# Both gates of a gated feed-forward layer by seven block products instead of eight, with the steps behind attention in a written order

## Chip, core and metric

The kernel runs on one core of a Trainium2 chip. The metric is device time in microseconds (us) of one execution; of several executions the median counts.

## What is computed

Attention with rotary positions (2 batches, 8 heads, 576 positions, 64 per head), a gated layer, and a layer with a softmax-weighted activation and a normalisation. Cut to what matters:

```python
x = attention(q, k, v)                 # as 1152 rows of 512
a = x @ w_a                            # 512 -> 1536
b = x @ w_b                            # 512 -> 1536
x = (a * b) @ w_out                    # 1536 -> 512
h = x @ w_in                           # 512 -> 1024
e = np.exp(h - np.max(h, axis=-1, keepdims=True))
solu = h * (e / (np.sum(e, axis=-1, keepdims=True) + 1e-09))
ln = (solu - mean(solu)) / np.sqrt(var(solu) + 1e-06) * g_ln
return ln @ w_out2                     # 1024 -> 512
```

The weights arrive as 64-bit floats.

## The kernel before

**Precision.** Each operand of a matmul is split into a high part (rounded to the matmul's own float32 form) and a low part (the rest); a product is three matmuls, high by high, high by low and low by high, summed in PSUM.

**Weights.** A 64-bit weight tile is loaded on SP's queue into `raw` (two staging buffers, each with its `f`), and `pack` makes a float32 tile of its bits in five steps: step 0 (L89, absolute value) on ACT; step 1 (L91, clip to a range), step 2 (L93, shift), step 3 (L95, sign) and step 4 (L97, low bits) on DVE. `high` (L103) rounds on ACT, `low` (L106) subtracts on POOL or on DVE. A staging buffer is loaded again when step 4 has read it.

**Attention** (up to about 167 us) runs by positions in a table (`PLAN` and its variants); what interests here is that it ends with `x_last`, which writes the last columns of `xT`: four tiles of 128 features by 1152 positions, high and low. The two batches are columns 0 to 575 and 576 to 1151. The first two of twelve weight blocks, and eight of the matmul triples of block 0, stand inside that table.

**Gates** (L629 to L646). The 1536 columns of `w_a` and `w_b` are cut in 12 blocks of 128. For block `f` and column third `t` (384 positions) one group of 24 matmuls fills two PSUM banks: 2 gates, 4 feature tiles, 3 matmuls each. ACT copies gate a out (L637), DVE multiplies it by gate b (L638), ACT and DVE split the product into `gT` (L645, L646). Two groups are open at a time. Steps of later weight blocks are dealt out between the groups.

**The second matmul** (L745): for each of 4 output tiles and each third, all 12 blocks are summed, 36 matmuls of 384 columns in a row; `x2_out` splits the result. **The last layer**: `hmm` (L792, 24 matmuls of 512 columns for each of 9 row tiles), a chain of maximum, exponential, product, statistics and norm, four-fold transposes (L834), the output matmuls (L863) and the stores. Here the order is written out by hand.

Engines take their instructions in the order of the program; a step waits by semaphores for what it reads and for the buffer that it writes.

Of the kernel before, what the change touches and what calls it, by code (L numbers as in the profile page):

```python
# [75 lines left out]
class Weights:  # L76
# [3 lines left out]
    def __init__(self, nc, raw, t, w, scale=None):  # L80
        self.nc, self.raw, self.t, self.w, self.scale = nc, raw, t, w, scale

    def pack(self, steps=range(5)):

        eng, t = self.nc.vector, self.t
        lo, hi = self.raw[:, :, 0], self.raw[:, :, 1]
        for step in steps:
            if step == 0:
                self.nc.scalar.activation(_raw(t), _raw(hi), AF.Abs)  # L89
            elif step == 1:  # L90
                eng.tensor_scalar(_raw(t), _raw(t), LOW_END, HIGH_END, op0=ALU.max, op1=ALU.min)  # L91
            elif step == 2:
                eng.tensor_scalar(t, t, 3, 0x3FFFFFFF, op0=ALU.logical_shift_left, op1=ALU.bitwise_and)  # L93
            elif step == 3:
                eng.scalar_tensor_tensor(t, hi, -(1 << 30), t, op0=ALU.bitwise_and, op1=ALU.bitwise_or)  # L95
            else:
                eng.scalar_tensor_tensor(t, lo, 29, t, op0=ALU.logical_shift_right, op1=ALU.bitwise_or)  # L97

    def high(self):
        t = _raw(self.t)  # L100
        if self.scale is not None:
            self.nc.scalar.activation(t, t, AF.Copy, scale=self.scale)
        self.nc.scalar.copy(self.w[:, 0], t)  # L103
# [6 lines left out]
def attention_gated_ffn_solu_ffn(ctx: ExitStack, tc, q, k, v, wa, wb, wo1, wi2, wo2, gln, rope_cs, out):  # L110
# [17 lines left out]
    W, wt = {}, {}  # L128
# [7 lines left out]
    def load_w(key, w, raw, t):  # L136
        kind, n = key
        scale = None
        if kind == "ab":
            rv = raw.rearrange("p (m k c) t -> p m k (c t)", m=2, k=4)  # L140
            for m, src in enumerate((wa, wb)):
                nc.sync.dma_start(
                    out=rv[:, m], in_=src[:, 2 * n * P:2 * (n + 1) * P].rearrange("(k p) c -> p k c", p=P)
                )
        elif kind == "x":
            m, half = divmod(n, 2)
            raw, t = raw[:, :6 * P], t[:, :6 * P]
            nc.sync.dma_start(
                out=raw.rearrange("p (f c) t -> p f (c t)", f=6),
                in_=wo1[half * 6 * P:(half + 1) * 6 * P, 2 * m * P:2 * (m + 1) * P].rearrange("(f p) c -> p f c", p=P),  # L150
            )
        else:
            half = slice(n % 2 * DM, (n % 2 + 1) * DM)
            raw, t, w = raw[:, half], t[:, half], w[:, :, half]
            if kind == "h":
                t = staged[n // 4][:, n % 4]
                src = wi2[n // 2 * P:(n // 2 + 1) * P, n % 2 * 2 * DM:(n % 2 + 1) * 2 * DM]
            else:
                src, scale = wo2[n * P:(n + 1) * P, :], g_sb[:, n:n + 1]
            nc.sync.dma_start(out=raw.rearrange("p c t -> p (c t)"), in_=src)  # L160
        W[key] = Weights(nc, raw, t, w, scale)

    def wtile(pool, tag, key):
        return pool.tile([P, 2, 6 * P if key[0] == "x" else 8 * P], F32R, tag=tag, name=f"w{key[0]}{key[1]}")
# [456 lines left out]
    gT, pab = {}, {}  # L621

    def ab_some(f, t, m, ks):
        if (f, t) not in pab:
            pab[f, t] = ps_s.tile([P, 2, 512], F32, tag="s", name=f"ab{f}_{t}")
        wf = W["ab", f].w.rearrange("p a (m k c) -> p a m k c", m=2, k=4)
        for kk in ks:
            for a, xa in ((0, 0), (0, 1), (1, 0)):
                nc.tensor.matmul(  # L629
                    pab[f, t][:, m, :CW], wf[:, a, m, kk, :], xT[kk][:, xa, t * CW:(t + 1) * CW],  # L630
                    start=(kk == a == xa == 0), stop=(kk == 3 and a == 1),
                )

    def ab_mult(f, t):
        pr = pab.pop((f, t))
        a_sb = mt.tile([P, 512], F32, tag="row", name=f"a{f}_{t}")[:, :CW]
        nc.scalar.copy(a_sb, pr[:, 0, :CW])  # L637
        nc.vector.tensor_tensor(a_sb, pr[:, 1, :CW], a_sb, op=ALU.mult)  # L638
        return a_sb

    def ab_split(f, t, a_sb):
        if (f // 3, t) not in gT:
            gT[f // 3, t] = gpool.tile([P, 3, 2, CW], F32R, tag=f"g{t}{f // 3}", name=f"gT{t}_{f // 3}")
        g = gT[f // 3, t][:, f % 3]
        nc.scalar.copy(g[:, 0], a_sb)  # L645
        nc.vector.tensor_tensor(g[:, 1], a_sb, _raw(g[:, 0]), op=ALU.subtract)  # L646


    for f, loaded, steps in ((0, 54.0, W_POS[:6]), (1, W_POS[4] + 0.1, W_POS[6:])):
        key = ("ab", f)  # L650
        add(loaded, lambda key: load_w(key, wtile(w0, "w", key), raw0, f0), key)
        for i, pos in enumerate(steps[:5]):
            add(pos, lambda key, i: W[key].pack((i,)), key, i)
# [9 lines left out]
    fctx = ExitStack()  # L663
    ps_t = fctx.enter_context(tc.tile_pool(name="ps_t", bufs=2, space=PSUM))
    ps_o = fctx.enter_context(tc.tile_pool(name="ps_o", bufs=2, space=PSUM))
    mt = fctx.enter_context(tc.tile_pool(name="mt", bufs=2))
    wp = fctx.enter_context(tc.tile_pool(name="wp", bufs=2))
    gpool = fctx.enter_context(tc.tile_pool(name="gp", bufs=1))
    order = [("ab", f) for f in range(NF)] + [("x", n) for n in range(8)]
    order += [("h", n) for n in range(8)] + [("out", n) for n in range(8)]  # L670
    NW, NX = len(order), NF + 8
    raw1, f1 = buffers(wp)

    def load_n(n):
# [260 lines left out]
```

## Time and profile before

| | |
|---|---|
| median of 3 runs | 501.54 us (501.2 to 502.69) |
| the profiled execution | 502.1 us, of which the span in the profile is 500.3 us |
| PE busy | 485.2 us, 97% of the span |
| DVE busy | 374.3 us, 75% |
| ACT busy | 268.7 us, 54% |
| POOL busy | 150.8 us, 30% |
| instructions | 7965 |

PE is the TensorE matmul queue and PEld its weight loads, which run beside it. DVE, ACT, POOL and SP are the vector, scalar, GpSimd and sync engines. "Idle before" and "waited for" tell what ended an engine's idle time. The chain of waits follows the work back from the last instruction.

### The profile page before, as it was taken

The page shows a single profiled execution, that of the slowest core. Times are in us where ns is not written, and L with a number is a line of the kernel's source. Part 1 is how long each engine was busy: PE and PEld are TensorE (multiplying, and loading weights), DVE is VectorE, ACT ScalarE, POOL GpSimd, SP SyncE. Part 2 cuts the span into 40 slices and gives each one's busy share as a digit, 9 for nine tenths or more (in the row PEclk, how much of TensorE's full clock was granted, in tenths as well). Part 3 has the DMA queues.
Part 4 walks back from the last instruction along what each step waited for, and adds up shares of the span by engine and source line. Part 5 has one row for each costly group of instructions (what it writes and reads, how often), then busy time and mean ns, then how long its engine had stood idle before and what let it go on. Part 6 is the DMA issues. An engine that isn't in the chain of part 4 may idle for free.

```text
span 500.3 us, 7965 instructions
## 1 busy us (share of the span) xinstructions
PE 485.2 (97%) x3008; PEld 458.8 (92%) x3008; DVE 374.3 (75%) x603; ACT 268.7 (54%) x564; POOL 150.8 (30%) x118
## 2 busy tenths in 40 slices
PE   7699999999999999999999999999999999999997
PEld 7589999999988999999999999999999988888886
DVE  5589999999999577666756656689789898755551
ACT  3789999999988344343433433342347434222221
POOL 1997999987305002111111221100000000000000
PEclk9999999999999999999999999999999999999999
DMA  4413423424102243222232121263453100000011
GB/s 113 112 50 98 120 53 99 114 57 135 51 25 85 90 134 114 86 84 85 86 100 97 66 95 64 67 228 128 168 170 126 43 0 22 21 23 21 23 42 42
DMA packets 50804, 41.72 MB, mean 83 GB/s; under 512 B 23695, under 2 KB 46798, under 8 KB 50766
## 3 DMA queue, kind: packets, MB, share of 16 engines
q1 hardware_dynamic: 49882, 40.33, 26.5%
q10 hardware_dynamic: 884, 0.89, 0.5%
q8 instruction: 23, 0.38, 0.3%
q14 instruction: 15, 0.12, 0.1%
HBM read 36.92 MB, written 2.39 MB: 79 GB/s over the span
## 4 chain that ended last, share of the span: by engine, by line
PE 79%; DVE 8%; ACT 5%; POOL 4%; DMA 2%; issue 2%; SPq 0%; ACTq 0%; POOLq 0%; DVEq 0%
PE ab L629 28%; PE x L745 15%; PE out L863 10%; PE h L792 10%; PE pv L433 4%; PE s L354 4%; PE t L384 4%; DVE pT L402 2%; DVE nm L363 2%; PE lt L834 2%; ACT e L371 1%; ACT pT L398 1%; DVE x L447 1%; DMA kraw<-in_k_dram 1%; DMA qd<-in_q_dram 1%
## 5 line engine op out<-in xcount | busy, mean ns | idle before, releaser
L629 PE MATMUL ab<-xT,wab 128*128 128x384 f32 x864 | 151.4, 334 | 0.3 <-DVE a L638 0.3
L629 PEld LDWEIGHTS ab<-xT,wab 128*128 128x128 f32 x864 | 149.5, 188 | 0.6 <-DVE a L638 0.6
L745 PE MATMUL x<-gT,wx 128*128 128x384 f32 x432 | 75.2, 334 | 0.0
L745 PEld LDWEIGHTS x<-gT,wx 128*128 128x128 f32 x432 | 74.9, 188 | 0.1
L354 PE MATMUL s<-kS,qS 128*128 128x288 f32 x320 | 59.3, 311 | 3.6 <-ACT e L371 3.6
L106 POOL TENSOR_TENSOR wab<-f,wab 128x1024 fp32r<-128x1024 f32 x11 | 26.4, 2400 | 120.4 <-ACT wab L103 104.5
L371 ACT ACTIVATE e<-s,nm 128x576 f32<-128x576 f32 x72 | 53.5, 744 | 4.7 <-DVE nm L363 4.6
L402 DVE TENSOR_TENSOR pT<-t,pT 128x512 fp32r<-128x512 f32 x72 | 49.6, 688 | 7.6 <-ACT pT L398 6.2
L363 DVE TENSOR_REDUCE nm<-s 128x1 f32<-128x576 f32 x72 | 53.8, 748 | 1.1 <-PE s L354 1.1
L863 PE MATMUL out<-wout,lnT 128*128 128x512 f32 (+1 forms) x240 | 52.7, 372 | 0.0
L820 POOL TENSOR_TENSOR rs<-mv,mhalf 128x1 f32<-128x1 f32 x9 | 5.3, 586 | 154.8 <-DVE mv L818 154.8
L354 PEld LDWEIGHTS s<-kS,qS 128*128 128x128 f32 x320 | 45.9, 190 | 5.7 <-ACT e L371 5.2
L433 PE MATMUL pv<-pT,V 128*128 128x288 f32 x288 | 50.6, 302 | 0.2 <-DVE pT L420 0.2
L863 PEld LDWEIGHTS out<-wout,lnT 128*128 128x128 f32 x240 | 41.3, 189 | 7.4 <-DVE wout L106 0.2
L384 PE MATMUL t<-ident,e 128*128 128x128 f32 x288 | 44.3, 277 | 0.8
L398 ACT CAST pT<-t 128x512 fp32r<-128x512 f32 x72 | 41.8, 581 | 2.5 <-PE t L384 2.0
L433 PEld LDWEIGHTS pv<-pT,V 128*128 128x128 f32 x288 | 41.4, 188 | 0.7 <-POOL xT L501 0.4
L646 DVE TENSOR_TENSOR gT<-a,gT 128x384 fp32r<-128x384 f32 x36 | 23.5, 651 | 21.9 <-ACT gT L645 21.9
L637 ACT COPY a<-ab 128x384 f32<-128x384 f32 x36 | 17.3, 480 | 41.2 <-PE ab L629 40.6
L645 ACT CAST gT<-a 128x384 fp32r<-128x384 f32 x36 | 18.5, 514 | 37.4 <-DVE a L638 37.4
L384 PEld LDWEIGHTS t<-ident,e 128*128 128x128 f32 x288 | 34.0, 142 | 3.3 <-DVE pT L402 2.2
L805 ACT ACTIVATE et<-h,mx 128x1024 f32<-128x1024 f32 x9 | 10.1, 1118 | 47.8 <-DVE mx L804 47.8
(141 smaller groups left out, 739.1 us busy)
## 6 DMA issues: line engine op xcount, KB each, us to landing
raw<-in_moe_w_a_dram SPq DMA_DIRECT2D x12, 512.0 KB
raw<-in_moe_w_b_dram SPq DMA_DIRECT2D x12, 512.0 KB
raw<-in_moe_w_out_dram SPq DMA_DIRECT2D x8, 768.0 KB
raw<-in_moe_w_in_dram SPq DMA_DIRECT2D x8, 512.0 KB
raw<-in_moe_w_out_dram SPq DMA_DIRECT2D x8, 512.0 KB
kraw<-in_k_dram SPq DMA_DIRECT2D x16, 128.0 KB
qd<-in_q_dram SPq DMA_DIRECT2D x16, 128.0 KB
vraw<-in_v_dram SPq DMA_DIRECT2D x8, 256.0 KB
```

What stands on the lines that cost most here:

```text
L106: eng.tensor_tensor(self.w[:, 1], _raw(self.t), _raw(self.w[:, 0]), op=ALU.subtract)
L354: nc.tensor.matmul(s[:, c, :KC], qS[u % 2][:, a, off:off + P], kS[u % 2][:, h, c * KC:(c + 1) * KC], start=(m == 0), stop=(m == last),)
L363: nc.vector.tensor_reduce(t, ps[n][:, :, :KC], axis=AX.XY, op=ALU.max, negate=True)
L371: nc.scalar.activation(t.rearrange("p (c n) -> p c n", c=2), ps.pop(n)[:, :, :KC], AF.Exp, bias=nm.pop(n), accum_out=sums[u][:, i:i + 1],)
L384: nc.tensor.transpose(t[:, j, :], e[n][:, j * P:(j + 1) * P], ident)
L398: nc.scalar.copy(hi, src)
L402: nc.vector.tensor_tensor(lo, src, _raw(hi), op=ALU.subtract)
L433: nc.tensor.matmul(o[:, :KC], w[:, h, 4 if m == 8 else m % 4].rearrange("p a d -> p (a d)"), t[:, m, c * KC:(c + 1) * KC], start=(m == 0), ...
L629: nc.tensor.matmul(pab[f, t][:, m, :CW], wf[:, a, m, kk, :], xT[kk][:, xa, t * CW:(t + 1) * CW], start=(kk == a == xa == 0), stop=(kk == 3 ...
L745: nc.tensor.matmul(o[:, :CW], wx[:, a], gT[f // 3, t][:, f % 3, ga], start=(f == 0 and a == ga), stop=(f == NF - 1 and a == 1),)
L792: nc.tensor.matmul(s[:, c], x2T[kk][:, xa, c0:c0 + P], wt["h", kk][:, a, c * 512:(c + 1) * 512], start=(idx == 0), stop=(idx == 11),)
L863: nc.tensor.matmul(o[:, cols], t[:, la, kk, :], w[:, a, cols], start=(kk == la == a == 0), stop=(kk == NK2 - 1 and la == 1),)
```

## The change

Blocks 0, 1 and 2 of the gates are computed as before, in the three column thirds. For blocks 3 to 11 the pair of gates is one product of two by two blocks: rows are gate a and gate b, the inner dimension is cut in two halves of 256 features, the columns are the two batches. It is formed by Strassen's method in Winograd's form: seven products (`P1` to `P7`) of 12 matmuls with 288 columns, 84 matmuls where there were 72 with 384 columns.

- Four sums of `xT`'s blocks are made once, in float32, and split (`s1` to `s4`, `sb`, `sh`, `sl`); one of them replaces batch 0 of `xT`'s tiles 0 and 1.
- Four sums of weight blocks are made for each block (`t1`, `t2`, `t4`) and split into `wT`; the three plain blocks that are used go to `wB`.
- The products are gathered in three pairs of PSUM banks: `a` and `c` with one buffer, `b` with two. ACT copies `a` after `P1` into `b` (`o1`), and copies results out of the banks between products (`o7`, `o6`, `o2`); DVE adds (`o4`, `o5`) and forms the gated product in float32 (`g1`, `g0`).
- The gated product `g` is kept in float32 and split shortly before use, in a ring of three (`gh`, `gl`). The second matmul takes the blocks `f` outermost: one step `X` is 12 matmuls, 4 output tiles by 3, of 384 columns; two thirds are open at a time.
- The clip of `pack` on DVE is replaced: ACT takes the absolute value with a large scale and scales back in two more copies (`pa`, `pb`, `pc`), for weight tiles 2 and later. All `low` steps of tiles 2 and later stand on DVE; POOL keeps the one power of each row tile.
- A weight load for the gates is three DMAs instead of two, of the same bytes. Tiles of the second matmul and of the last layer are loaded in pieces of 1024 columns.
- Everything after attention is issued in the order of one table of words, `SCHEDULE`.

The core of the diff:

```diff
+NSTD = 3
+SCHEDULE = """
+AB.0.1 ab.0.0 s1.1 g.0.0 AB.0.2 ab.0.1 p3.1 g.0.1 p4.1 hi.1 ld.2 s1.0 lo.1 pa.2 pb.2 ab.0.2 pc.2 ld.3 sb.0.0
...
+    def pack(self, step):
...
+        if step == "a":
+            act.activation(_raw(t), _raw(hi), AF.Abs, scale=2.0 ** SHIFT)
+        elif step in ("b", "c"):
+            act.activation(_raw(t), _raw(t), AF.Copy, scale=2.0 ** -SHIFT)
...
-            for m, src in enumerate((wa, wb)):
+            for src, k0, k1, at_ in ((wa, 0, 4, 0), (wb, 2, 4, 4), (wb, 0, 2, 6)):
...
+    def s1_a(k, eng=0):
+        tt_(f_slot(0, k), _raw(x_part(k, 0)), _raw(x_part(2 + k, 0)), plus, eng)
...
+    def t_sum(j):
+        def fn(f, eng=0):
...
+                T1: (t[:, 0:2], w[:, B12:B21:-1], w[:, B11::B12]), T2: (t[:, T2], w[:, B22], t[:, T1]),
+                T4: (t[:, T4], w[:, B21], t[:, T2]),
...
+    def product(name, w_of, x, fresh=False):
+        def fn(f):
+            if fresh:
+                bank_of[name, f] = ps_a.tile([P, 2, 512], F32, tag=name, name=f"p{name}{f}")
+            (ws, q), dst = w_of, bank_of[name, f]
+            w = ws[f][:, :, q]
+            for c in range(2):
+                for k in range(2):
+                    for a, xa in ((0, 0), (0, 1), (1, 0)):
+                        nc.tensor.matmul(
+                            dst[:, c, :KC], w[:, a, k * P:(k + 1) * P], x(k, xa)[:, c * KC:(c + 1) * KC],
+                            start=(fresh and k == a == xa == 0), stop=(k == 1 and a == 1), skip_group_check=True,
+                        )
...
+    def seed_b(f):
+        bank_of["b", f] = ps_s.tile([P, 2, 512], F32, tag="s", name=f"pb{f}")
+        nc.scalar.copy(bank_of["b", f][:, :, :KC], bank_of["a", f][:, :, :KC])
...
+    def add_u2(f):
+        nc.vector.tensor_tensor(two(u2[f]), bank_of.pop(("c", f))[:, :, :KC], two(u2[f]), op=plus)
...
+    def g1_mult(f):
+        dst = two(g_tile(f)[:, f % 6, S:])
+        nc.vector.tensor_tensor(dst, bank_of.pop(("b", f))[:, :, :KC], two(c11.pop(f)), op=mul)
...
+    def g_hi(t, f):
+        parts[t, f] = r = ring.tile([P, 2, 512], F32R, tag="g", name=f"gs{t}_{f}")[:, :, :CW]
+        nc.scalar.copy(r[:, 0], g[f // 6][:, f % 6, t * CW:(t + 1) * CW])
...
+    def x_mm(t, f):
+        r = parts.pop((t, f))
+        for m in range(4):
...
+            for a, ga in ((0, 0), (0, 1), (1, 0)):
+                nc.tensor.matmul(
+                    px[t, m][:, :CW], w[:, a], r[:, ga], start=(f == 0 and a == ga),
+                    stop=(f == NF - 1 and a == 1),
+                )
...
+    for word in SCHEDULE.split():
+        name, *args = word.split(".")
+        STEP[name](*map(int, args))
```

A word is a step, its block or tile, and its third or half: `AB.0.1` are the 24 matmuls of block 0 and third 1, `P7.3` the seventh product of block 3.

PE at the start of block 3 in the program of before; `ab` is a group's PSUM, `wab` a weight block, `xT_71` to `xT_74` the four tiles of `xT`:

```order
L629 MATMUL ab_2_2858<-xT_74,wab_2602 128x384 x3
L629 MATMUL ab_0_2890<-xT_71,wab_2610 128x384 x3
L629 MATMUL ab_0_2890<-xT_72,wab_2610 128x384 x3
L629 MATMUL ab_0_2890<-xT_73,wab_2610 128x384 x3
L629 MATMUL ab_0_2890<-xT_74,wab_2610 128x384 x3
```

And PE where block 3's products follow block 2's last group in the changed program; `pa`, `pb`, `pc` are the bank pairs, `sums_x` the split sums of `xT`:

```order
L676 MATMUL ab_2_2911<-xT_74,wab_2757 128x384 x3
L864 MATMUL pc_2944<-sums_x,wT_2892 128x288 x12
L864 MATMUL pa_2839<-xT_73,wB_2827 128x288 x3
L864 MATMUL pa_2839<-xT_74,wB_2827 128x288 x3
L864 MATMUL pa_2839<-xT_73,wB_2827 128x288 x3
L864 MATMUL pa_2839<-xT_74,wB_2827 128x288 x3
L864 MATMUL pb_2936<-sums_x,wT_2892 128x288 x12
L864 MATMUL pc_2944<-xT_73,wT_2892 128x288 x3
```

Groups of 384 columns have become products of 288, and successive products go to different bank pairs (`P7`, `P2`, `P6`, `P4`; `P1` stands 48 matmuls earlier).

DVE right behind attention, before (`f` and `raw` are the weight staging, `a` and `gT` the gated product):

```order
L95 SCALAR_TENSOR_TENSOR f<-raw,f 128x1024
L638 TENSOR_TENSOR a_0_2606<-ab_0_2468,a_0_2606 128x384
L97 SCALAR_TENSOR_TENSOR f<-raw,f 128x1024
L646 TENSOR_TENSOR gT_0_2614<-a_0_2606,gT_0_2614 128x384
L106 TENSOR_TENSOR wab_2340<-f,wab_2340 128x1024
L638 TENSOR_TENSOR a_1_2643<-ab_1_2618,a_1_2643 128x384
L646 TENSOR_TENSOR gT_0_2646<-a_1_2643,gT_0_2646 128x384
L91 TENSOR_SCALAR f<-f 128x1024
```

And in the changed program (`sums_f` are the sums in float32, `g` the gated product):

```order
L714 TENSOR_TENSOR sums_f<-xT_72,xT_74 128x1152
L764 TENSOR_TENSOR g_2616<-ab_0_2470,a_0_2644 128x384
L147 SCALAR_TENSOR_TENSOR f<-raw,f 128x1024
L764 TENSOR_TENSOR g_2616<-ab_1_2619,a_1_2673 128x384
L149 SCALAR_TENSOR_TENSOR f<-raw,f 128x1024
L714 TENSOR_TENSOR sums_f<-xT_71,xT_73 128x1152
L159 TENSOR_TENSOR wab_2341<-f,wab_2341 128x1024
L714 TENSOR_TENSOR sums_f<-sums_f 128x576
L714 TENSOR_TENSOR sums_f<-xT_71 128x1152
L714 TENSOR_TENSOR sums_f<-sums_f,xT_71 128x576
L145 TENSOR_SCALAR f<-f 128x1024
```

The sums of `xT` stand between the steps of the weights, the splits of the gated product have left, and the low part of weight block 1 (`wab_2341`) comes after two sums.

DVE about one block of the gates in the later program, before:

```order
L638 TENSOR_TENSOR a_0_2915<-ab_0_2890,a_0_2915 128x384
L646 TENSOR_TENSOR gT_1_2918<-a_0_2915,gT_1_2918 128x384
L91 TENSOR_SCALAR f<-f 128x1024
L93 TENSOR_SCALAR f<-f 128x1024
L95 SCALAR_TENSOR_TENSOR f<-raw,f 128x1024
L638 TENSOR_TENSOR a_1_2950<-ab_1_2925,a_1_2950 128x384
L646 TENSOR_TENSOR gT_1_2953<-a_1_2950,gT_1_2953 128x384
L97 SCALAR_TENSOR_TENSOR f<-raw,f 128x1024
```

And in the changed program, around the end of block 3 (`u` and `p` are the copied results that DVE adds to, `c` the one that it multiplies by):

```order
L888 TENSOR_TENSOR u_4_3106<-pc_3044,u_4_3106 128x576
L145 TENSOR_SCALAR f<-f 128x1024
L714 TENSOR_TENSOR wT_3109<-tf_3042,wT_3109 128x1024
L714 TENSOR_TENSOR wB_3126<-f,wB_3126 128x768
L895 TENSOR_TENSOR g_2616<-pb_2936,c_3_2974 128x576
L891 TENSOR_TENSOR p_4_3059<-pb_3057,p_4_3059 128x576
L147 SCALAR_TENSOR_TENSOR f<-raw,f 128x1024
L149 SCALAR_TENSOR_TENSOR f<-raw,f 128x1024
L898 SCALAR_TENSOR_TENSOR g_2616<-u_4_3106,p_4_3059 128x576
```

The steps that free a bank pair (`L888`, `L891`, `L895`) stand in one queue with the sums, the low parts and the packing of two other blocks.

## Rows read from the trace of the kernel before

**Rows 1.** The page's busy times of the engines: us, share, instructions.

```profile
PE 485.2 (97%) x3008; PEld 458.8 (92%) x3008; DVE 374.3 (75%) x603; ACT 268.7 (54%) x564; POOL 150.8 (30%) x118
```

**Rows 2.** Busy time of each engine in stretches, with granted clock and DMA.

```profile
190.00:314.00 124.00, 124.00 (x718) 124.00 (x717) 80.61 (x106) 50.59 (x82) 25.31 (x11) 1.00 0.26 85
314.00:390.00 76.00, 76.00 (x432) 75.02 (x432) 62.86 (x103) 32.52 (x54) 1.85 (x1) 1.00 0.45 153
```

**Rows 3.** The chain of waits from the gates on: start, us, what.

```profile
177.28 137.55 PE ab L629 x792
314.84 68.64 PE x L745 x396
...
430.89 5.44 PE h L792 x24
```

**Rows 4.** All waits of PE on one releaser: us, times, longest.

```profile
PE ab L629 <- DVE a L638: 0.3, 1, 0.3
```

**Rows 5.** Timeline of PE in attention: start, us, matmuls of 288 and 128 columns.

```profile
118.80 0.69 PE L354 MATMUL s<-kS,qS 128*128 128x288 f32 x4
119.33 0.69 PE L433 MATMUL pv<-pT,V 128*128 128x288 f32 x4
119.86 0.60 PE L384 MATMUL t<-ident,e 128*128 128x128 f32 x4
120.21 0.91 PE L433 MATMUL pv<-pT,V 128*128 128x288 f32 x5
120.96 0.69 PE L354 MATMUL s<-kS,qS 128*128 128x288 f32 x4
```

**Rows 6.** The page's costliest groups: weight loads of three shapes of matmul.

```profile
L629 PEld LDWEIGHTS ab<-xT,wab 128*128 128x128 f32 x864 | 149.5, 188 | 0.6 <-DVE a L638 0.6
L433 PEld LDWEIGHTS pv<-pT,V 128*128 128x128 f32 x288 | 41.4, 188 | 0.7 <-POOL xT L501 0.4
L384 PEld LDWEIGHTS t<-ident,e 128*128 128x128 f32 x288 | 34.0, 142 | 3.3 <-DVE pT L402 2.2
```

**Rows 7.** Timeline behind attention: DVE, ACT and PE, start and us.

```profile
167.43 9.53 PE L629 MATMUL ab<-xT,wab 128*128 128x384 f32 x54
169.62 0.46 DVE L511 TENSOR_TENSOR xT<-x,xT 128x288 fp32r<-128x288 f32 x1 [0.50 <-ACT xT L510]
175.54 1.22 DVE L106 TENSOR_TENSOR wab<-f,wab 128x1024 fp32r<-128x1024 f32 x1
176.68 0.55 DVE L638 TENSOR_TENSOR a<-ab,a 128x384 f32<-128x384 f32 x1
```

**Rows 8.** Groups of instructions by line and shape: us, mean ns.

```profile
L638 DVE TENSOR_TENSOR a<-ab,a 128x384 f32<-128x384 f32 x30 | 16.6, 555 | 17.5 <-ACT a L637 17.3
L637 ACT COPY a<-ab 128x384 f32<-128x384 f32 x30 | 14.4, 481 | 38.1 <-PE ab L629 38.1
L95 DVE SCALAR_TENSOR_TENSOR f<-raw,f 128x1024 int32<-128x1024 int32 x9 | 11.0, 1221 | 0.1
L103 ACT CAST wab<-f 128x1024 fp32r<-128x1024 f32 x9 | 9.5, 1050 | 5.3 <-DVE f L97 5.3
L106 DVE TENSOR_TENSOR wout<-f,wout 128x512 fp32r<-128x512 f32 x8 | 5.4, 686 | 0.7 <-ACT wout L103 0.7
L106 DVE TENSOR_TENSOR wx<-f,wx 128x768 fp32r<-128x768 f32 x5 | 4.7, 957 | 2.3 <-ACT wx L103 2.3
L363 DVE TENSOR_REDUCE nm<-s 128x1 f32<-128x576 f32 x72 | 53.8, 748 | 1.1 <-PE s L354 1.1
L371 ACT ACTIVATE e<-s,nm 128x576 f32<-128x576 f32 x72 | 53.5, 744 | 4.7 <-DVE nm L363 4.6
```

**Rows 9.** Timeline of a weight block's packing beside POOL's low part.

```profile
276.03 2.41 POOL L106 TENSOR_TENSOR wab<-f,wab 128x1024 fp32r<-128x1024 f32 x1 [10.07 <-ACT wab L103]
276.97 2.02 DVE L91 TENSOR_SCALAR f<-f 128x1024 f32<-128x1024 f32 x1 [1.43 <-ACT f L89]
279.02 0.69 DVE L93 TENSOR_SCALAR f<-f 128x1024 int32<-128x1024 int32 x1
```

More of the change, by code (lines that the diff above doesn't have):

```diff
@@ new lines, in tt_, with pack, home @@
+    def tt_(out_, a, b, op, eng=0):
+        (nc.vector, nc.gpsimd)[eng].tensor_tensor(out_, a, b, op=op)
+    queue = [("ab", f) for f in range(NF)]
+    queue += [("x", n) for n in range(6)] + [("h", n) for n in range(4)] + [("out", n) for n in range(4)]
+    def load_n(n):
+        load_w(queue[n], None, *((raw1, f1), (raw0, f0))[n % 2])
+    def pack(step):
+        return lambda n: W[queue[n]].pack(step)
+    def home(n):
+        kind, m = queue[n]
+        if kind == "out" and m < 3:
+            if m == 0:
+                pools["wo"] = gpool.tile([P, 3, 2, 8 * P], F32R, tag="g0", name="wo")
+            return pools["wo"][:, m]
+        if queue[n] in (("ab", 1), ("ab", 2), ("x", 0), ("x", 2), ("h", 3), ("out", 3)):
+            pool, tag = w0, "w"
+        elif queue[n] in (("ab", 3), ("x", 1)):
+            pool, tag = wxp, "w"
+        else:
+            pool, tag = pools["x" if kind == "x" else "h"], f"{kind}{m}"
+        return pool.tile([P, 2, 8 * P], F32R, tag=tag, name=f"w{kind}{m}")
@@ new lines, in high, with low, scaled, ab_pe @@
+    def high(n):
+        w = W[queue[n]]
+        if w.w is None:
+            w.w = home(n)
+        w.high()
+    def low(n, eng=0):
+        W[queue[n]].low((nc.vector, nc.gpsimd)[eng])
+    def scaled(n, j):
+        W[queue[n]].scaled(j)
+    def ab_pe(f, t):
+        for m in range(2):
+            ab_some(f, t, m, range(4))
+    a_sb = {}
+    def ab_act(f, t):
+        a_sb[f, t] = mt.tile([P, S], F32, tag="row", name=f"a{f}_{t}")[:, :CW]
+        nc.scalar.activation(a_sb[f, t], pab[f, t][:, 0, :CW], AF.Copy, scale=UP ** -2 if f > 1 else 1.0)
@@ new lines, in t_lo, with b_hi, b_lo, two @@
+    def t_lo(f, eng=0):
+        tt_(wT[f][:, 1], tf.pop(f), _raw(wT[f])[:, 0], sub, eng)
+    def b_hi(f):
+        wB[f] = wbp.tile([P, 2, 3, 256], F32R, tag="wb", name=f"wB{f}")
+        nc.scalar.copy(wB[f][:, 0], blocks(f)[:, 0:3])
+    def b_lo(f, eng=0):
+        tt_(wB[f][:, 1], blocks(f)[:, 0:3], _raw(wB[f])[:, 0], sub, eng)
+    bank_of, c11, u2, p7 = {}, {}, {}, {}
+    def two(t):
+        return t.rearrange("p (c n) -> p c n", c=2)
+    def sum_of(j):
+        return lambda k, a: sums_x[:, j, k, a]
```

469 lines of the change are left out of this document (255 added, 214 removed).

## The prediction

> **What bounds the kernel now.** I read the engines' busy times first: PE is busy for 485.2 of 500.3 us and DVE for 374.3 [rows 1]. A share over the whole span may hide stages, so next the stretches: from 190 to 390 us PE is busy for the whole of each stretch at the full granted clock, with DVE at 65% and 83%, ACT at 41% and 43% [rows 2]. The chain of waits says the same: from 177.28 us on it is one piece of 792 gate matmuls, then 396 of the second layer, then the last layer [rows 3], and in all of the gates PE waits once, for 0.3 us [rows 4]. So time is gained here only by fewer or shorter matmuls, and lost by whatever makes PE wait. Idle time of DVE, ACT and POOL is worth nothing until one of them falls behind PE.
>
> **The matmuls.** 792 gate matmuls take 137.55 us, 173.7 ns each [rows 3]. A block has 72 of them: 12.51 us; nine blocks 112.5 us. They become 9 x 84 = 756 matmuls of 288 columns. That shape stands in attention: four `s` matmuls start at 118.80 and the next kind at 119.33, four `pv` from 119.33 to 119.86, so 132.5 ns each [rows 5]. From the other side, 24 matmuls of 512 columns take 5.44 us, 226.7 ns each [rows 3]; the line through 512 and 384 columns has 0.414 ns per column and gives 133.9 ns at 288. I take 133 ns: a block costs 11.17 us, nine cost 100.5 us, and **12.0 us are saved**. The near ends are 12.4 (132.5 ns) and 11.3 us (133.9 ns). The far end is the five `pv` matmuls from 120.21 to 120.96, 150 ns each [rows 5]; at that price nine blocks cost 113.4 us, 0.9 us more than now. I don't take it, since the first of these five follows transposes, and the four behind a matmul of their own kind show no such excess; it is kept as a rival. No row shows a stretch as long as 756 matmuls, the longest pure run here is thirteen.
>
> On this term the Trainium skill, "TensorE: Matmul & The Clock Gate", section "Back-to-back issue gap", gives columns over 2.4 GHz and 2.5 ns more; by it the saving would be 9 x (72 x 162.5 - 84 x 122.5 ns) = 12.7 us, an estimate from that page. The rows have about 13 ns on top of the columns, not 2.5, and a fixed part is paid 84 times instead of 72, which is why I stay lower.
>
> The other matmuls keep number and shape: the second layer's 432 of 384 columns come in another order, as do the last layer's. The last copy and store follow the same two halves of the last row tile, so I leave the end alone.
>
> **Where the work of the seven products lies.** DVE has, per block: step 2 of packing 0.69 [rows 9]; steps 3 and 4, 2 x 1.22 [rows 8]; weight sums of 512 (0.69) and twice 256 columns (at most 0.46 each, the row for 288 [rows 7]); the low parts of 1024 (1.22) and 768 columns (0.96) [rows 7, 8]; four operations on 576 columns, at 0.75 by the row that reads as many from PSUM [rows 8]. That is 9.9 us beside 11.2 us of PE. Neighbours that don't depend on each other overlap: the 1.22 us row at 175.54 is followed at 176.68 [rows 7], 0.08 less; with twelve of them, 8.9 us. So DVE goes from 65% to 80 or 89%, and is still hidden. What it no longer does is the clip, which cost it up to 2.02 us beside POOL's low part [rows 9]; POOL is silent in this stage, so no such row should appear. ACT has three passes of packing and the roundings of 1024 and 768 columns, five at 1.05 or less, and four copies of 576, 0.74 at most [rows 8]: some 8.2 us of 11.2, also hidden. If DVE's cover went, its surplus over 11.2 us would go on the path nine times.
>
> **The entry.** Here DVE has most to do. The four sums of `xT` cost four operations on 1152 columns (1.35 each, extended from 768 and 1024 columns) and twenty on 576: 20.4 us, all wanted within 52 us of PE work, on top of packing.
> - Weight block 1: DVE finishes `xT` at 170.08 [rows 7]; a sum 1.35, a gate product 0.56, step 3 1.22, then a product that waits for group 0.1 (30 of the 54 matmuls from 167.43 [rows 7] end at 172.64, ACT's copy 0.48 [rows 8], the product 0.56, with semaphores 173.8), step 4 to 175.0. The rounding on ACT (1.05) runs beside another sum, to 176.35; the low part ends near 177.6. Before, PE restarted at 177.28 [rows 3]. Cost **0.3 us**; queued behind the wait is all of PE.
> - First use of a sum: `P7` of block 3. PE gets there at 204.2 (177.55 plus six groups of 4.17 and `P1`, 1.60). DVE must have done 42 instructions since 170.08, the durations above add up to 36.3 us: 206.4 if none overlap, 203.0 if all do. By full durations the next such points cost 0.2 (`P6`), 0.6 (`P7` of block 4) and 0.4 us (`P3` of block 3), in all 3.4; by overlapping ones nothing. Rows of both kinds stand there, so I take the middle, rounded down: **1.5 us**.
>
> **The pairs of banks.** `a` and `c` have one buffer, so a product often waits until the previous content was copied. One copy is 0.75 us, a product 1.6 us. In the order at least one other product stands between writer and next writer, so 1.6 us cover 0.75 and the semaphores; cost 0. If a copy stands behind one 1.22 us operation in DVE's queue the cover is used up (1.97 against 1.6), and PE and everything behind it waits 0.4 us.
>
> **The second layer.** An `X` step is 12 x 173.3 ns = 2.08 us. Its operand needs a copy (0.48) and a subtraction (0.56 [rows 8]) shortly before, two steps ahead, so 4.2 us cover 1.1 plus one long operation in the queue: cost 0; a step without cover would cost 1.1 us. DVE now has all low parts, but it loses the clip there too. Loads: the same bytes with DMA at 26% and 45% [rows 2], one or two blocks ahead; a third DMA issue per gate tile stands on SP's queue, where only later loads follow. Cost 0 to 1 us, taken as 0.
>
> **Sum.** -12.0 + 0.3 + 1.5 = -10.2 us. The profiled execution took 502.1 us (span 500.3), which gives 491.9; the median of runs is 0.56 us below it, so the forecast for a median is 501.54 - 10.2 = **491.3 us**, with its own range 488.8 to 494.0 (12.4 saved and no entry stall, with half a microsecond for scatter; 11.3 saved and 3.4 us of stall).
>
> **Rivals.**
> - DVE keeps PE waiting beyond the entry. For it: up to 89% in one queue, with waits on ACT between a rounding and its low part. Against it: 1.3 to 2.3 us to spare in each block. One missed cover of 0.4 us and one of 0.2 per block make 9 x 0.6 = 5.4 us: about 496.7, range 494 to 500.
> - **Slower: bank pairs handed over one by one.** If the copies out of `a` and `c` were reached late every time, because DVE's queue holds two long operations ahead of each, a handover would cost 0.75 + 2 x 1.22 - 1.6 = 1.6 us. One such handover per block gives 9 x 1.6 = 14.4 us and 505.7. It decides at 10.2/9 = 1.1 us of PE idle per block. Against it speaks the order, where the steps that free banks stand ahead of packing as often as behind.
> - 150 ns per matmul also in long runs: +0.9 + 1.8, 504.2 us. It decides at 112.5/756 = 149 ns.
> - Slower by weight loads: each matmul has a load, 149.5 us for 864, 173 ns [rows 6]. Were that a floor, 756 loads would take 130.8 us against 112.5, and the run 501.54 + 18.3 + 1.8 = 521.6 us. But the loads of `pv` add up to 144 ns each, those of the transposes to 118 [rows 6], and a `pv` comes every 132.5 ns [rows 5]: the load stretches with the matmul beside it.
>
> To that last rival belongs a rule: the Trainium skill, "Trainium Kernel Development and Optimization", section "Performance Expectations", tells a reader to judge by the busy share of the weight loads and not by matmul time. Read so, a change that adds loads to an engine with 92% of them would be a mistake. The rows on `pv` speak against it.
>
> **Chances.** Forecast 0.60; DVE beyond the entry 0.24; handovers 0.08; 150 ns 0.04; loads 0.04. That the change doesn't form seven products is not open, the order shows 84 matmuls per block. A measurement of this kernel can tell about 0.3%, 1.5 us, from no change. The first two cases are faster by more: 0.84. Of the other three, 0.03 falls within 0.3% and 0.13 is slower. The range leaves out the last three cases and the top of the second: 488.8 to 498.5.
>
> **What would show it.** Right: products spaced by 132 to 134 ns, DVE at about 8 or 9 tenths through the products, PE idle for under 4 us behind attention, most of it within 50 us after it. Wrong: matmuls at 150 ns or more; PE waiting on DVE or ACT for bank pairs in every block; waits on the gate's splits among the `X` steps.

## The result, and the profile of the changed kernel

| | median of runs | kernel before, beside it | ratio |
|---|---|---|---|
| changed kernel | 489.03 us (488.73 to 489.92) | 501.61 us | 0.9749, 95% interval 0.9729 to 0.9769 |
| the same, another session | 489.72 us (489.38 to 490.09) | 501.80 us | 0.976, 0.9738 to 0.9781 |

It is faster by 12.6 and 12.1 us, where 10.2 were forecast. The profiled execution took 488.92 us with a span of 487.1, 13.2 less than before; the granted clock was 1.000 of full speed.

The page's busy times, to be set beside [rows 1]:

```profile
PE 472.4 (97%) x3116; PEld 446.2 (92%) x3116; DVE 400.7 (82%) x612; ACT 332.9 (68%) x618; POOL 121.2 (25%) x105
```

PE is as dense as it was, with 108 matmuls more in 12.8 us less. The stretches (us busy of PE, PEld, DVE, ACT, POOL, with counts; granted clock, DMA share, GB/s), to be set beside [rows 2]:

```profile
220.00:260.00 40.00, 40.00 (x304) 40.00 (x303) 36.05 (x47) 27.40 (x34) 0.00 (x0) 1.00 0.28 90
260.00:305.00 45.00, 45.00 (x335) 45.00 (x335) 38.97 (x50) 30.84 (x39) 0.00 (x0) 1.00 0.31 108
305.00:380.00 75.00, 75.00 (x427) 73.99 (x426) 62.04 (x83) 59.89 (x84) 0.00 (x0) 1.00 0.39 141
```

Through the products PE has no gap, DVE has gone from 65% to 90 and 87%, and POOL is silent. The chain of waits (start, us, what), beside [rows 3]:

```profile
176.68 16.57 PE ab L676 x94
...
203.16 1.58 PE pc L864 x12
...
301.94 58.24 PE x L932 x336
```

PE's timeline where the dense part behind attention starts (start, us, what), beside its row in [rows 7]:

```profile
166.50 9.90 PE L676 MATMUL ab<-xT,wab 128*128 128x384 f32 x56
176.68 16.57 PE L676 MATMUL ab<-xT,wab 128*128 128x384 f32 x94 [0.28 <-DVE wab L159]
```

From 176.68 on it is PE alone. A product of twelve matmuls takes 1.593 us: 62 of them lie between 203.16 and 301.94. That is 132.8 ns per matmul. From the start of the dense part to the second layer it is 301.94 - 166.50 = 135.44 us, where before it was 314.84 - 167.43 = 147.41 [rows 3, 7]: **12.0 us** less. (Counted from PE's restart behind its one wait, 125.3 stands against 137.55 [rows 3], 12.3 less; but at that restart PE has done 56 matmuls of the dense part where it had done 54, and two are 0.35 us.) The rest of the 13.2 us lies at both ends. The dense part starts 0.9 us earlier (in the second profile of the same kernel it starts at 167.68, so this is scatter of attention, whose code is the same); and from the second layer to the end it is 185.2 instead of 185.5 us. PE waits on a releaser behind attention as often as in [rows 4], once, for 0.28 us at 176.68, now for the low part of weight block 1.

### The profile page after: what moved, and what is told of

Same layout as the page of the kernel before. It is cut to its first block, busy times and chain, and to the rows that moved or that the text cites. A ratio compares the mean times of both kernels' runs of the same rounds, so it can differ in the third digit from the quotient of the medians.

```text
span 487.1 us, 8244 instructions
## 1 busy us (share of the span) xinstructions
PE 472.4 (97%) x3116; PEld 446.2 (92%) x3116; DVE 400.7 (82%) x612; ACT 332.9 (68%) x618; POOL 121.2 (25%) x105
## 4 chain that ended last, share of the span: by engine, by line
PE 80%; DVE 8%; POOL 4%; ACT 4%; issue 2%; DMA 2%; ACTq 0%; DVEq 0%; POOLq 0%
PE x L932 15%; PE h L956 10%; PE out L1033 10%; PE pb L864 9%; PE pa L864 6%; PE pc L864 6%; PE ab L676 6%; PE pv L480 5%; PE s L401 5%; PE t L431 4%; DVE pT L449 2%; PE lt L997 2%; DVE nm L410 1%; DVE x L494 1%; ACT pT L445 1%
## 5 line engine op out<-in xcount | busy, mean ns | idle before, releaser
L932 PE MATMUL x<-gs,wx 128*128 128x384 f32 x432 | 75.6, 334 | 0.0
L932 PEld LDWEIGHTS x<-gs,wx 128*128 128x128 f32 x432 | 75.0, 188 | 0.3
L956 PE MATMUL h<-wh,x2T 128*128 128x512 f32 x216 | 52.5, 395 | 0.0
L139 ACT ACTIVATE f<-f 128x1024 f32<-128x1024 f32 x48 | 50.9, 1061 | 1.1
L956 PEld LDWEIGHTS h<-wh,x2T 128*128 128x128 f32 x216 | 39.8, 188 | 7.9
L676 PE MATMUL ab<-xT,wab 128*128 128x384 f32 x216 | 39.3, 336 | 0.3 <-DVE wab L159 0.3
L1033 PE MATMUL out<-wo,lnT 128*128 128x512 f32 (+1 forms) x180 | 39.1, 370 | 0.0
L676 PEld LDWEIGHTS ab<-xT,wab 128*128 128x128 f32 x216 | 37.2, 188 | 0.6 <-DVE wab L159 0.6
L1033 PEld LDWEIGHTS out<-wo,lnT 128*128 128x128 f32 x180 | 31.3, 189 | 5.4
L147 DVE SCALAR_TENSOR_TENSOR f<-raw,f 128x1024 int32<-128x1024 int32 x26 | 31.7, 1220 | 0.5
L149 DVE SCALAR_TENSOR_TENSOR f<-raw,f 128x1024 int32<-128x1024 int32 x26 | 31.7, 1221 | 0.4
```

The costliest lines, as they stand in the source:

```text
L139: act.activation(_raw(t), _raw(t), AF.Copy, scale=2.0 ** -SHIFT)
L676: nc.tensor.matmul(pab[f, t][:, m, :CW], wf[:, a, (kk, 4 + (kk + 2) % 4)[m], :], xT[kk][:, xa, t * CW:(t + 1) * CW], start=(kk == a == xa ...
L932: nc.tensor.matmul(px[t, m][:, :CW], w[:, a], r[:, ga], start=(f == 0 and a == ga), stop=(f == NF - 1 and a == 1),)
L956: nc.tensor.matmul(ph[i][:, c], x2T[kk][:, xa, i * P:(i + 1) * P], W["h", kk].w[:, a, c * 512:(c + 1) * 512], start=(kk == xa == a == 0), ...
L1033: nc.tensor.matmul(po[i, part][:, cols], lnT[i][:, la, kk, :], w[:, a, cols], start=(kk == la == a == 0), stop=(kk == NK2 - 1 and la == 1),)
```

## The experiments

Every kernel below is the changed kernel with one edit. Their times are set against **489.4 us**, half-way between the unchanged kernel's two medians, and differences under 1 us are not read. The kernel before stood at 502.3, 502.2 and 501.8 us in the three sessions of these runs, and at 501.6 beside the result; the unchanged kernel was run again only in the third, so some tenths between sessions stay in the differences. Four prices recur in them, and the table at the end adds them up: a matmul's 132.8 ns, PE's waits, what a wait costs on top, and a lower clock behind a long wait.

### An eighth product: is it the columns or the weight loads that set the spacing?

```diff
-P7.3
+P7.3 P8.3
...
+    def again(f):
+        product("c", (wT, T3), sum_of(2), None)(f)
```

> The changed kernel with P7 of every block formed twice (the second starts the banks afresh, so the result stays): 9 x 12 more matmuls of 288 columns. Theory A, PE alone sets the time: 9 x 1.593 = +14.3 us, 503.4 us, above the kernel before. Rival, DVE or the handover of banks sets part of the time and more PE work fills gaps: under +12 us. Rival, a weight load of 173 ns is a floor: +18.7 us.

Measured: 503.6 us, +14.2, with no wait of PE that the changed kernel doesn't have. That is 108 matmuls at 131.5 ns. A floor of 173 ns per weight load is refuted, and the 12.2 us by which 648 matmuls of 384 columns (173.7 ns) and 756 of 288 differ have a second witness that owes nothing to another schedule.

### The plain groups in place of the products

The same table of steps, with the nine blocks formed by plain groups as before; first at the places where three of the products stood (words of block 5; in the table other steps stand between them):

```diff
-P7.5 P4.5 P5.5 bh.5 bl.5
+AB.5.0 ab.5.0 g.5.0 AB.5.1 ab.5.1 g.5.1 AB.5.2 ab.5.2 g.5.2 hi.5 lo.5
```

> The changed kernel with blocks 3 to 11 as plain groups again (three groups of 24 matmuls of 384 columns each), without the sums; its written order, the float32 gates, the ring of split gates, the second layer with depth outermost, ACT's scaling in place of the clip and the low parts on DVE stay. Theory A, the gain is the matmuls alone: nine blocks go from 84 x 132.8 ns = 11.15 us to 12.51 us, so +12.2 us, 501.2 us, with at most 0.5 us of waits. Rival, part of the gain comes from the order and the other edits: clearly under 501, about 498 if a quarter of it does.

Measured: 507.59 us, +18.2, six too many. The groups had come out unevenly spaced, and PE's waits on one releaser (us, times, longest) show it:

```profile
PE x L927 <- DVE wx L154: 1.6, 1, 1.6
PE ab L671 <- DVE g L759: 1.5, 2, 1.2
PE x L927 <- ACT gs L906: 0.6, 1, 0.6
PE x L927 <- ACT wx L151: 0.6, 1, 0.6
```

As a test of the products alone this decided nothing, so the groups were dealt out again with the weight steps evenly between them (here block 8):

```diff
-P7.8 P4.8 P5.8
+AB.8.0 ab.8.0 g.8.0 p3.10 AB.8.1 ab.8.1 g.8.1 p4.10 ld.12 hi.10 lo.10 AB.8.2 ab.8.2 g.8.2
```

> Blocks 3 to 11 as plain groups again, as in plain_order, but with the weight steps dealt out evenly between the 35 groups as in the kernel before, and odd pairs of weight blocks in the space that the sums had, so that no group waits for its weights; everything from the second layer on as in the changed kernel. Theory A, the gain is the matmuls alone and the 4.5 us of PE waits in plain_order came from its uneven order: 489.0 + 12.2 = 501.2 us, waits of PE behind attention under 1 us. Rival, the other edits give part of the gain or take from it: 499 or less, or 503 or more, without PE waits to account for it.

Measured: 504.51 us, +15.1, 3.3 us above theory A. All gates are now one piece without a wait, and two waits are left where the second layer starts:

```profile
PE x L930 <- DVE gs L709: 1.1, 1, 1.1
PE x L930 <- ACT gs L909: 0.9, 1, 0.9
```

12.2 for the matmuls, 2.0 for these waits and 0.5 on top of them (below) make 14.7. So the reordering, the float32 `g` and the depth-outermost second layer save nothing that can be measured by themselves, with plain groups: the gain is the products'. What the products do need is an order in which nobody waits, and the plain order at their places shows that it doesn't come for free.

### A product less: is PE the only bound?

```diff
-P3.3
...
-P3.11
```

> The changed kernel without P3 of every block, so one half of the gates lacks one of its terms (left out: a twelfth-part sum of each of these blocks, the output is not the reference's). Theory A, PE alone sets the time and DVE's cover still holds at 9.56 us of PE per block: -14.3 us, 474.7 us. Rival, DVE becomes the bound at about 10 us per block: nine times 1.1 us less than now, -10 to -11 us, about 478.5 us, with PE waiting on DVE in most blocks.

Measured: 485.44 us, only 4.0 less, though 14.3 us of matmuls are gone; neither theory had that. PE's waits, and one of them in the chain (start, us, what):

```profile
PE pa L864 <- ACT pb L873: 3.4, 4, 1.0
PE x L932 <- ACT c L885: 2.3, 1, 2.3
PE pc L864 <- DVE wT L714: 0.8, 1, 0.8
PE pb L864 <- ACT u L881: 0.8, 1, 0.8
```

```profile
233.16 1.61 PE pa L864 x12
234.77 0.02 issue
234.79 0.63 ACT pb L873
235.42 0.04 issue
235.47 1.86 PE pa L864 x12
```

The most frequent is not DVE but a bank pair: `P2` writes the pair `a` that ACT has to copy after `P1` (step `o1`), and the `P3` of the block before, which stood between them, is gone. Two things are to be read from the chain. The handover itself is 0.7 us of idle PE, and the chain counts 1.86 us for the product behind it where it counts 1.59 for one in an unbroken row, so a wait costs **0.27 us on top of itself** (the next experiment shows of what).

### Bank pairs handed over bare

This asks the same of the full kernel: without less work, is it the product between that hides a handover? `o7` and `P4` are put directly behind `P7` in the blocks 5 to 11.

```diff
-P7.7 pa.9 pb.9 pc.9 o7.7 th.8 p2.9 P3.6 g1.6 bh.8 bl.8 P6.7 o6.7 P2.7 o2.7 P4.7
+P7.7 o7.7 P4.7 pa.9 pb.9 pc.9 th.8 p2.9 P3.6 g1.6 bh.8 bl.8 P6.7 o6.7 P2.7 o2.7
```

> For the column blocks 5 to 11 the steps o7.f and P4.f stand directly behind P7.f, so that the product P4 takes the banks that P7 has just left and nothing lies between them: PE has to sit out the copy of 576 columns that o7 makes. Nothing is left out and no work is added. Theory A (a handover costs nothing only because a product of 1.59 us stands between): seven bare handovers, each 0.63 to 0.75 us for the copy, 0.1 us for the two crossings and 0.27 us for the slow start of the next product, about 1.0 us each: 7 us over the unchanged kernel, about 496.4, with a wait of PE for ACT o7 of 0.7 to 0.9 us seven times. The rival of the prediction priced a bare handover at 1.6 us: 11 us, about 500.5. Theory B (the other bank pairs or PE's queue cover it all the same): under 2 us.

Measured: 500.93 us, +11.5, and 0.9982 (0.9968 to 0.9996) of the kernel before: nearly all of the gain gone, with the same 84 matmuls per block.

```profile
PE pc L864 <- ACT p L877: 5.1, 7, 0.8
PE pb L864 <- ACT u L881: 2.3, 3, 0.8
PE pa L864 <- ACT c L885: 0.7, 1, 0.7
```

```profile
222.84 1.60 PE pc L864 x12
224.44 0.02 issue
224.46 0.65 ACT p L877
225.11 0.04 issue
225.16 1.85 PE pc L864 x12
```

The same in PE's timeline:

```profile
222.67 1.75 PE L864 MATMUL pc<-sums_x,wT 128*128 128x288 f32 x12
225.16 1.85 PE L864 MATMUL pc<-xT,wT 128*128 128x288 f32 x12 [0.73 <-ACT p L877]
226.85 1.76 PE L864 MATMUL pa<-xT,wB 128*128 128x288 f32 x12
```

The price of one handover is as theory A had it: 0.73 us of wait (ACT's copy and two crossings) and 0.26 on top, 1.0 together. From start to start, since the profile models the ends of matmuls: 226.85 - 222.67 = 4.18 us, where two products take 3.19. Of the 0.26, 0.16 is overlap: products of 1.75 us start every 1.59 us, so each starts before the one ahead has ended, and the one behind a wait doesn't. The other 0.10 is the product itself, 1.69 us from its start to the next one's. Theory A's total was too low: there are eleven handovers, not seven. `P4` had also stood between `P6` and `P5`, which share the pair `b` (`u`, three waits), and once between `P2` and the next `P1` (`c`). Eleven times 1.0 is 11.2. The rival's 1.6 us each would have come close to the total, by a wrong price and a wrong count.

### How much DVE can still take

Steps that only keep DVE busy, ahead of `p3` of the tiles 7 to 13: two additions of 512 columns in one kernel (688 ns each, 9.6 us in all) and four in another (19.3 us).

```diff
-p3.8
+dd dd p3.8
...
+    def more_dve():
+        nc.vector.tensor_tensor(idle, idle, idle, op=plus)
```

> The changed kernel with four more DVE additions of 512 columns (0.69 us each, 0.61 from start to start) ahead of step 3 of weight tiles 7 to 13, on a tile that no other engine touches: 2.4 us per block in seven blocks. By the changed kernel's trace DVE is idle 1.1 to 1.5 us of the 11.15 us of a block. Theory A, DVE has only that idle time to give: 7 x (2.4 - 1.3) = +7.7 us, 496.7 us, PE waiting on DVE. Rival, the sum of non-overlapping durations (9.9 us of 11.2) misjudged DVE and 2.2 us are free: +1 to +2 us.

> Ahead of step p3 of the tiles 7 to 13 VectorE makes two extra additions of 512 columns that depend on each other, some 1.4 us per block (0.70 us each in the run with four); nothing is left out. Theory S (VectorE can give up only about 0.5 us per block behind attention, whatever its idle share says): 0.9 us times 7, about 6 us over the unchanged kernel, 495. Theory I (what is idle can be used, 1.1 to 1.5 us per block): 0 to 2 us over it, 489 to 491, and the +15 of the run with four additions was the price of a few long waits with a lower clock behind them.

Measured: four additions 504.71 us, +15.3; two additions 493.38 us, +4.0. In the stretches above DVE is idle for 10 to 13%, 1.1 to 1.5 us of the 11.15 us of a block. In kernel time the two kernels took in 5.6 of 9.6 and 4.0 of 19.3 us, 0.8 and 0.6 us per block. These are estimates, since 1.1 and 3.8 us of what was lost are in the table below what PE pays behind its waits. DVE's busy time from 203 to 302 us points the same way: 88.7 of 99 us in the changed kernel, 92.8 with two additions and 92.3 with four, so 4.1 and 3.6 of 10.3 idle us were filled. DVE could use roughly half of what it shows as idle. The rest lies where it waits for a product, as in this group of the changed kernel (busy us, mean ns, idle before and what ended it), nine instructions with 6.1 us of idle time ahead of them:

```profile
L888 DVE TENSOR_TENSOR u<-pc,u 128x576 f32<-128x576 f32 x9 | 6.8, 755 | 6.1 <-PE pc L864 6.1
```

The first expectation's +7.7 was short by half, and its rival's +1 to 2 by more; of the second, +4.0 lies half-way between its +6 and the upper end of its 0 to 2, and decides for neither. PE's waits in the products with two additions:

```profile
PE pa L864 <- DVE wB L714: 1.4, 1, 1.4
PE pc L864 <- DVE u L888: 0.5, 1, 0.5
PE pb L864 <- DVE p L891: 0.3, 1, 0.3
```

They are the low part of a weight block and the two additions that free a bank pair, places at which PE stands directly behind DVE's queue.

### The low part back on POOL

```diff
-tl.7
+tl.7.1
```

> The changed kernel with the low part of the weight sums (wT, 1024 columns, 1.22 us on DVE) of blocks 3 to 11 on POOL, where such a step took 2.40 us before. Theory A, PE alone sets the time and covers hold: 489.0 us within 0.8, some 0.5 us at the first P7, which now waits 1.2 us longer. Rival, POOL and DVE hinder each other as in the kernel before (a clip of 2.02 us beside POOL instead of 0.69): DVE falls behind and PE waits, 491 us or more.

Measured: 493.33 us, +3.9, as the rival had it. Taking 1.22 us per block off DVE made the kernel slower. Groups from 165 to 310 us (busy us, mean ns, idle before), then one step on both engines (start, us, what):

```profile
L714 POOL TENSOR_TENSOR wT<-tf,wT 128x1024 fp32r<-128x1024 f32 x9 | 24.6, 2734 | 110.0 <-ACT wT L831 110.0
L149 DVE SCALAR_TENSOR_TENSOR f<-raw,f 128x1024 int32<-128x1024 int32 x14 | 22.8, 1632 | 0.2
```

```profile
202.11 2.69 POOL L714 TENSOR_TENSOR wT<-tf,wT 128x1024 fp32r<-128x1024 f32 x1 [43.48 <-ACT wT L831]
202.58 3.31 DVE L149 SCALAR_TENSOR_TENSOR f<-raw,f 128x1024 int32<-128x1024 int32 x1
```

DVE's step 4, 1.22 us in the changed kernel, takes 3.31 us when it starts beside POOL's subtraction and 1.63 on the mean. POOL needs 2.73 us for what takes DVE 1.22. The Trainium skill, "SBUF — State Buffer", section "Who interferes with whom", says that a VectorE instruction with two SBUF inputs contends with a GpSimd instruction that reads SBUF. These rows agree: both have two inputs in SBUF, and the one that came second ends at 205.89, 1.1 us after POOL's end at 204.80, about as if it had begun there. So it went with all seven steps of DVE with two inputs in SBUF that started beside one of the nine subtractions; they end 0.4 to 1.1 us after it. The four of step 4, two low parts of `wB` and one split of `g` grew by 5.7, 2.7 and 2.2 us, 10.6 us in all, where nine times 1.22, 11.0 us, had been taken off: DVE has gained next to nothing, and the low parts come later.

With `P3` left out as above and the low part on POOL:

```diff
-P3.7
...
-tl.7
+tl.7.1
```

> six_products (P3 of every block left out, so the output lacks those terms) and the low part of the weight sums on POOL. Theory H, six_products lost its gain to handovers of bank pairs, because P3 no longer stands between P1 and P2: DVE's relief changes nothing, 485.4 us within 1.5. Rival D, DVE's queue was what bound six_products: 1.1 us less on DVE per block gives back up to 9 us, 476 to 480 us.

Measured: 494.26 us, as neither theory had it: far above the 485.4 with six products alone and, as its executions range from 490.81 to 495.41, not to be told from the 493.3 with the low part on POOL alone. PE has twelve waits behind attention beyond the unchanged kernel's, 11.7 us: the bank pairs' of the kernel with six products and, of 2.3 and 2.1 us, those for the low parts on POOL and DVE. What the test was to tell, whether relief of DVE gives the six products their time back, it can't: POOL is no relief.

### The entry, delayed

Four dependent additions (2.8 us) are put into DVE's queue ahead of the first sum that the products need.

```diff
-s2a.1
+dd dd dd dd s2a.1
```

> The changed kernel with four more DVE additions of 512 columns, one after the other on a tile of their own (2.8 us in all), just ahead of s2a.1, so before the first use of block 3's plain weights. Theory A, DVE has 0.3 to 0.5 us to spare at the entry, as its trace shows, and everything behind it moves: +2.3 to +2.6 us, 491.5 us, with PE waiting at the first P1 and P7. Rival, the entry has cover that the running sum doesn't show: no change.

Measured: 494.0 us, +4.6. PE's timeline (start, us, what; in brackets the wait) and the granted clock behind it (last three columns: clock, DMA share, GB/s):

```profile
194.78 0.42 PE L864 MATMUL pa<-xT,wB 128*128 128x288 f32 x2
197.52 1.60 PE L864 MATMUL pa<-xT,wB 128*128 128x288 f32 x10 [2.32 <-DVE wB L714]
198.96 10.05 PE L676 MATMUL ab<-xT,wab 128*128 128x384 f32 x48
```

```profile
196.00:198.00 2.00, 0.48 (x3) 0.48 (x4) 2.00 (x3) 1.37 (x3) 0.00 (x0) 1.00 0.00 0
198.00:200.00 2.00, 2.00 (x13) 2.00 (x12) 2.00 (x4) 1.94 (x3) 0.00 (x0) 0.75 0.00 0
200.00:202.00 2.00, 2.00 (x8) 2.00 (x7) 2.00 (x5) 1.55 (x2) 0.00 (x0) 0.50 0.00 0
202.00:204.00 2.00, 2.00 (x12) 2.00 (x12) 2.00 (x4) 0.05 (x1) 0.00 (x0) 0.90 0.00 0
```

The wait is about what was expected, 2.8 less the margin. What was not is the rest: the granted clock falls to 0.50 (the 1.2 GHz level) behind it, and the 48 matmuls that take 8.48 us in this view of the unchanged kernel take 10.05, **1.6 us** for the clock. The same dip stands behind the wait of 3.65 us with four additions and behind the 2.29 us with six products; behind the 1.41 us with two additions the clock stays at 1.00. The length of a wait alone doesn't decide it: one of 2.0 to 2.2 us at 22 us, in attention, stands in all thirteen profiles, and in two of them (the kernel before and the uneven plain groups) the clock fell to 0.50 behind it, in the others it didn't. Nor is the clock the same in all executions of a kernel: of the four with six products one had a mean clock of 1.000 and took 483.45 us, the others had 0.995 to 0.996 and took 485.39 to 485.91.

### The sum of the prices

Differences to 489.4 us. Products: 12 matmuls by nine blocks (14.3), or 12.2 for the plain groups. Waits: those of PE behind attention beyond the 0.3 us that the unchanged kernel has, with their number. On top: 0.27 us per wait. Clock: 1.6 us per dip. The last column leaves out attention and the last layer, where nothing was changed: it is the time from the start of the dense part to the first matmul of the last layer in the profile, less the 193.52 us that the changed kernel takes for it (193.53 in its second profile). From there to the end all of them take 127.1 us.

| edit | products | waits | on top | clock | sum | measured | in the profile |
|---|---|---|---|---|---|---|---|
| eighth product | +14.3 | 0 | 0 | 0 | 14.3 | +14.2 | +14.3 |
| plain, uneven | +12.2 | 4.4 (6) | 1.6 | 0 | 18.2 | +18.2 | +18.1 |
| plain, even | +12.2 | 2.0 (2) | 0.5 | 0 | 14.7 | +15.1 | +14.4 |
| six products | -14.3 | 7.2 (7) | 1.9 | 1.6 | -3.6 | -4.0 | -3.6 |
| bare handovers | 0 | 8.2 (11) | 3.0 | 0 | 11.2 | +11.5 | +11.0 |
| two additions | 0 | 2.3 (4) | 1.1 | 0 | 3.4 | +4.0 | +3.8 |
| four additions | 0 | 10.5 (8) | 2.2 | 1.6 | 14.3 | +15.3 | +15.4 |
| low part on POOL | 0 | 1.8 (3) | 0.8 | 0 | 2.6 | +3.9 | +3.1 |
| both | -14.3 | 11.7 (12) | 3.2 | 3.2 | 3.8 | +4.9 | +3.5 |
| entry delayed | 0 | 2.5 (2) | 0.5 | 1.6 | 4.6 | +4.6 | +4.7 |

The prices were read in the rows of six products (0.27) and of the delayed entry (1.6), so these two don't test them; the others do. In the profile nine of ten sums agree within 0.5 us. The four additions miss by 1.1: three pauses of PE of 0.09 to 0.14 us, too short for the list of waits, cost 1.2 us there from start to start, and one such pause 0.4 us in the kernel with the low part on POOL. The even plain groups lie 0.3 below their sum, as they don't have the unchanged kernel's wait of 0.3. Against the medians the largest misses are 1.3 and 1.1 us; the profiled executions scatter by up to 1.2 us in where attention ends.

## Why the prediction was right, and where its sizes were off

**The matmuls.** 133 ns was forecast, 132.8 measured; 12.0 us were to be saved, and 12.0 lie between the start of the dense part and the second layer. The near row, four matmuls of the same shape in attention [rows 5], gave the price to 0.2%, and the five at 150 ns were rightly not taken. By the formula in the Trainium skill's "Back-to-back issue gap" in "TensorE: Matmul & The Clock Gate", which that section gives for an isolated matmul, it would have been 122.5 ns, an estimate from that page; the measurement decides, and stands 10 ns above it.

**Weight block 1** was mis-sized: +0.3 us forecast, none measured. The low part arrives when it was expected, 7.5 us after DVE is done with `xT` (its subtraction starts at 175.41 and takes 1.22, so 176.63, and DVE's last row of `xT` ends at 169.15; forecast 177.6 and 170.08), and PE restarts 10.18 us after the dense part's start, where it was 9.85. But the prediction let all of block 1 wait for it. Only the third matmul of a group of three reads the low part, so PE has done two matmuls more by then (56, where [rows 7] have 54), and these are worth 0.35 us.

**The entry** is the larger term that was mis-sized: 1.5 us forecast, none measured. DVE's rows there and the two products of PE that they feed (start, us, what):

```profile
192.04 0.95 DVE L714 TENSOR_TENSOR wB<-f,wB 128x768 fp32r<-128x768 f32 x1
192.91 0.75 DVE L714 TENSOR_TENSOR sums_f<-xT,sums_f 128x576 f32<-128x576 f32 x1
...
201.47 1.22 DVE L714 TENSOR_TENSOR wT<-tf,wT 128x1024 fp32r<-128x1024 f32 x1
202.60 1.22 DVE L149 SCALAR_TENSOR_TENSOR f<-raw,f 128x1024 int32<-128x1024 int32 x1
```

```profile
193.09 1.75 PE L864 MATMUL pa<-xT,wB 128*128 128x288 f32 x12
203.00 1.75 PE L864 MATMUL pc<-sums_x,wT 128*128 128x288 f32 x12
```

The next row of DVE starts 0.08 to 0.09 us before the one above it ends, nearly everywhere. The prediction held rows of both kinds and took the middle; in a queue this full nearly all neighbours overlap, and the chain of work ends with the low part of `wT` at 202.69. `P7` starts at 203.00 and reads it in its third matmul, at about 203.26: 0.57 us to spare. The prediction also looked at the wrong place. A tighter place is the low part of block 3's `wB`, which ends at 192.99, while the third matmul of `P1` comes at about 193.35, 0.36 us later; and it was there, behind two matmuls of `P1`, that the delayed entry made PE wait, and not at `P7`.

**DVE in the products** was right in the sum (8.9 to 9.9 us per block; 10.0 and 9.7 measured) and hidden as forecast. "1.3 to 2.3 us to spare in each block" was too much: 1.1 to 1.5 are idle, and 0.6 to 0.8 could be filled. The rival that DVE keeps PE waiting didn't occur, but with two additions per block the kernel lost its 0.6 us per block (4.0 over seven).

**The clip and POOL.** POOL is silent in the products and DVE's rows have their undisturbed lengths, as forecast; the step that was given back to POOL in the experiment cost DVE about as much as it took off.

**The bank pairs.** Cost 0 was right, and the reason given for it (one product of 1.6 us covers a copy of 0.75) is shown: where the product between goes, 1.0 us appears each time. The slower rival had the right mechanism and a price too high by half, 1.6 us against 1.0, because no handover stood behind two long DVE operations; ACT makes the copies that decide it, in 0.65 us. Its point of decision, 1.1 us per block, was sound: eleven handovers, 11.2/9 = 1.2 us per block by the table, bring the kernel back to within 0.2% of the one before.

**The second layer and the loads.** 336 matmuls in 58.24 us are 173.3 ns each, without a wait: cost 0, as forecast.

**The sum.** The forecast was 2.3 us above the median: 1.5 for the entry, 0.3 for weight block 1, 0.3 in the last layers, and the rest within scatter. Both stalls erred the same way, so nothing cancelled; 489.0 lies at the low end of the range, 488.8, which was worked out for no stall at the entry.

## What to carry over

A change that trades matmuls for work on other engines keeps its gain only through the order of the steps: count what stands between the last writer of a bank pair and its next one, and at each place where PE follows another engine's queue, compare when that queue ends with when PE arrives. Price a matmul of a shape by a row of that shape behind its own kind, and read an engine's idle share as an upper bound, of which about half could be filled here. Ask of an operand that comes late which matmul is the first to read it: those ahead of it run on. A wait cost more than its length here: 0.27 us for each, and 1.6 us more where the clock fell behind it.

## What the runs showed of the hardware

- A product of PE behind a wait took 1.85 to 1.87 us from start to end at a granted clock of 1.00, where products in an unbroken row took 1.75 and overlapped by 0.16. That is 0.26 us on top of the wait.
- Behind waits of PE of 2.29, 2.32, 2.33 and 3.65 us, and behind 1.98 with 0.71 close after it, the granted clock fell to 0.50 and came back to 1.00, about 1.6 us lost; behind 1.41, 1.57, 1.87 and 1.91 us and eleven of 0.7 it stayed at 1.00. Behind the wait of 2.0 to 2.2 us in attention it fell in two of thirteen profiles.
- 108 weight loads more cost nothing of their own: an added matmul with its load cost 131.5 ns, though the loads [rows 6] had added up to 173 ns each.
- DVE's operation of two inputs of 1024 columns went from 1.22 to 3.31 us beside a POOL subtraction of 2.69 us. Operations with one input in PSUM kept their 0.75 us beside POOL, and those of two inputs that had started ahead of it their 1.22 to 1.23.
